# Expert blocks of 512, 256 and 128 tokens in a fused attention and routing kernel, with routing begun three steps sooner and TensorE begun on products of the identity

## The chip, the cores and the metric

The kernel runs on one core of one Trainium2 chip. The metric is the device time of one execution in microseconds, as the median of several runs. A profiled execution gives, besides, the order of time on each engine. In the profile PE is TensorE's matmuls, PEld its weight loads, DVE is VectorE, ACT is ScalarE, POOL is GpSimd, SP is SyncE, which here only issues DMAs; a "q" behind a name is the engine's sequencer, which waits and issues. L310 is line 310 of the kernel.

## The reference

Two stages are computed in fp32. The first is a gated attention without softmax for 8 batches of 2496 tokens, with 64 features for scores and 256 for values. The second sends each of the 19968 tokens to one of 8 experts, chosen by its id, and each expert is a pair of matrices with a relu between.

```python
scores = (1/S) * z @ z.T            # per batch, S = 2496, z: S x 64
attn   = np.maximum(scores, 0) ** 2
x      = u * (attn @ v)             # S x 256
...
expert_idx = token_ids * 2654435761 % 8
for e in range(8):
    h = np.maximum(x[expert_idx == e] @ w1[e], 0)   # 256 -> 1024
    out[expert_idx == e] = h @ w2[e]                # 1024 -> 256
```

## The kernel before

**Attention** (lines 731 to 842) goes through 200 steps: batch, group of 2 x 256 queries (5 a batch, the last of 2 x 224), block of keys (5 a group). In a step TensorE makes scores (`score`, L228), or ACT's queue loads them back from where the mirrored block was stored (`recall`, L289), since scores are symmetric; VectorE makes four sums of them (`sums`, L261 to L264) and a transposed copy for the mirror (`mirror`, L272). Then `attend` (L310) multiplies by v with the seven block products of a 2 x 2 scheme in place of eight. At the end of a group `join` (L320 to L328) puts the seven results together, reading the banks that the next group's first products need. VectorE prepares two steps ahead of TensorE. The scores of steps 0 and 1 and the transposes of z (`turn_z`, L171) stand ahead of the loop; the first score product is the first work of TensorE.

**Routing** (`places`, L415 to L604) is a generator: from step 5 on, each step of the attention runs one piece of it, 19 in all. It loads the ids (L424), counts the tokens of each expert by matmuls and scans, shares them out into blocks (`share`), finds the expert of each block (`eb_i`) and the slot of each token (`row`). A block belongs to one expert. There are as many blocks of 512 as surely can be filled, NL = 32; what is left of each expert goes into NR = 35 blocks of 128, which may be partly filled. `fill` zeroes the slots of the small blocks.

**Between the two** the rows of x are put into `xg_dram` and fetched back (`put`, `fetch`), multiplied by u on VectorE (`multiply`, L374) and scattered by POOL to their slots in `x_dram` (`sort`, L395). The last group goes another way: `gate_late` transposes it on TensorE against the identity (L384), multiplies it from PSUM (L386), and sorts it. The most frequent expert comes first in the slots, so the first two blocks (`SURE`) are surely complete before the last rows are sorted; their x is loaded five steps before the end (L814), and turned (`turn_x`, L697 to L705) at the last two steps (L789).

**Experts** (L989 to L1021): in iteration i TensorE multiplies block i by w1 (`up_large`, L901, "U") while block i-1 is multiplied by w2 (`down_large`, L931, "D"), each by seven block products. Upwards a product stands for two halves of the hidden features, so there are 14 pieces of U in an iteration, and 7 of D. Small blocks use plain products ("u" with L954, "d" with L965); `SMALL` gives each iteration but the first one or two of them. "X" and "x" turn the x of the next blocks. The order of the pieces is written out in `ORDER` as a string; engines are in order, so that string is the order on TensorE, VectorE and ScalarE. In `products` the seven products come as 1, 6, 7, 5, 2, 3, 4. Product 2 adds into the bank of 1, product 3 into the bank of 5:

```python
        ps1 = made(1, None)
        nc.scalar.copy(p1, ps1)                       # L864
        nc.vector.tensor_add(u, p1, made(6, None))    # L866
        ps7 = made(7, None)
        ps5 = made(5, None)
        nc.vector.tensor_add(c21, u, ps7)             # L871
        nc.vector.tensor_add(c22, c21, ps5)           # L872
        made(2, ps1)
        made(3, ps5)                                  # then L879
        nc.vector.tensor_sub(c21, c21, made(4, None)) # L882
```

For U four sums follow on VectorE (L912 to L915) when the next piece of U is asked for. Upwards the banks are two that are held (products 1 and 5) and two for the others; downwards two held, one for the others (6, 7 and 4 in turn), and one (`any`) for the small blocks and the gate. SP issues the weights in the order of the program, after the x loads of the same iteration (`load_x`, L684; `load_w`, L717, L720, L724). POOL stores the rows of the output by their indices (L854).

Of the kernel before, what the change touches and what calls it, by code (L numbers as in the profile page):

```python
# [11 lines left out]
F32 = mybir.dt.float32  # L12
# [13 lines left out]
def kernel(  # L26
# [26 lines left out]
    BLK = 512  # L53
    TB = BLK // P
    NL = -(-(N - E * (BLK - 1)) // BLK)
    NR = (N - NL * BLK + E * (P - 1)) // P
    NB = NL + NR
    NS = NL * TB + NR
# [317 lines left out]
    def gate_late(b, g, o):  # L376

        x_sb = late.tile([P, 2, 2, D], F32, name="x_row")
        for q in range(2):
            ps = down_ps.tile([P, 2, D], F32, name="g_ps", tag="any")  # L380
            for t in range(2):
                m = keys(g, t)
                for i in range(DP):
                    nc.tensor.transpose(ps[0:m, t, ts(i, P)], o[:, i, q, ds(t * P, m)], ident[:])  # L384
                x, y = times_u(b, g, x_sb, q, t, m)
                nc.vector.tensor_mul(x, ps[0:m, t].rearrange("p (h i k) -> p i h k", h=DP, k=L), y)  # L386
                sort(b, g, x_sb, 2 * q + t)
            yield
# [26 lines left out]
    def places():  # L415

        with tc.tile_pool(name="route", bufs=1) as route:
# [31 lines left out]
            def fill():  # L449
                if unfilled:  # L450
                    c = unfilled.pop(0)
                    n = min(7, NR - c)
                    nc.sync.dma_start(
                        x_dram[ds(NL * BLK + c * P, n * P), :].rearrange("(c p) d -> p c d", p=P), zero[:].unsqueeze(1).to_broadcast([P, n, D]))

# [58 lines left out]
            upto = wpool.tile([P, E, C], F32, name="upto", tag="w")  # L514
# [10 lines left out]
            nc.vector.tensor_tensor_scan(upto[:].rearrange(flat_e), one[:].to_broadcast([P, E * C]), upto[:].rearrange(flat_e), 0.0,  # L525
                                         op0=OP.mult, op1=OP.add)
            yield
            nc.vector.tensor_add(rank[:], rank[:], upto[:])
# [21 lines left out]

            large, large_end = share(count, BLK, 0, NL, "large")
            in_large = route.tile([P, E], F32)
            nc.vector.tensor_scalar(in_large[:], large[:], float(BLK), None, op0=OP.mult)
            nc.vector.tensor_sub(count[:], count[:], in_large[:])
            small, small_end = share(count, P, P - 1, NR, "small")
# [3 lines left out]
            shift = route.tile([P, E], F32)  # L559
            nc.vector.tensor_sub(shift[:], large_end[:], large[:])  # L560
            nc.vector.scalar_tensor_tensor(shift[:], shift[:], float(BLK), first[:], op0=OP.mult, op1=OP.subtract)
            more = route.tile([P, E], F32)
            nc.vector.tensor_sub(more[:], small_end[:], small[:])
            nc.vector.tensor_scalar(more[:], more[:], float(P), float(NL * BLK), op0=OP.mult, op1=OP.add)
            nc.vector.tensor_add(first[:], first[:], in_large[:])
            nc.vector.tensor_sub(more[:], more[:], first[:])
            nc.vector.tensor_sub(more[:], more[:], shift[:])

            for end, b0, nb in ((large_end, 0, NL), (small_end, NL, NR)):
# [4 lines left out]
                eb = route.tile([1, max(NL, NR)], F32, name="eb")  # L576
# [9 lines left out]
            past = upto  # L586
            nc.vector.tensor_tensor(past[:], rank[:], each(first), op=OP.is_ge)
            yield
            nc.vector.tensor_mul(past[:], past[:], each(more))
            yield  # L590
            nc.vector.tensor_add(rank[:], rank[:], each(shift))
            yield
            nc.vector.tensor_add(rank[:], rank[:], past[:])
            yield
# [78 lines left out]
    def large(j):  # L673
        return j < NL

    def slot_tiles(j):
        return range(j * TB, (j + 1) * TB) if large(j) else range(NL * (TB - 1) + j, NL * (TB - 1) + j + 1)

    def load_x(j):
        n = len(slot_tiles(j)) * P  # L680
        xq[j] = gpool.tile([P, n // L, DP, L], F32, name="xq" if large(j) else "xqs")
# [4 lines left out]
    def turn_x(j):  # L686

        n = len(slot_tiles(j))
        if large(j):
            x = gpool.tile([P, 2, DP, 2 * P], F32, name="xT")  # L690
            t = gpool.tile([P, 4, 2 * P], F32, name="xs")
# [3 lines left out]
        m = min(2, n) * P // L  # L695
# [12 lines left out]
    def turn_x_at_once(j):  # L708
        for _ in turn_x(j):
            pass  # L710

    def load_w(j, m):

        e = nc.sync.value_load(eb_i[0:1, j:j + 1], min_val=0, max_val=E - 1)
        if large(j):
# [13 lines left out]
    order.__enter__()  # L729

# [42 lines left out]
    for i, (b, g, s) in enumerate(steps):  # L773
# [14 lines left out]
        if i >= len(steps) - SURE:  # L788
            turn_x_at_once(i - len(steps) + SURE)  # L789
# [18 lines left out]
        if i == len(steps) - NT:  # L808
# [4 lines left out]
            for j in range(SURE):  # L813
                load_x(j)  # L814
        if i >= 5 and not is_routed:
# [4 lines left out]
        elif is_routed:  # L820
            if fetched and i >= fetched[0][0] + (5 if i < len(steps) - NT else 2):
                rows = fetched.pop(0)[1]
                multiply(*rows)
# [13 lines left out]
        if i == len(steps) - 2:  # L837
            load_u(b, g, late)
            load_w(1, 0)
# [46 lines left out]
    def up_large(j):  # L886
# [3 lines left out]
        h = hpool.tile([P, 2, 2, FQ, 2 * P], F32, name="h")  # L890
        sums = hpool.tile([P, 3, FQ, 2 * P], F32, name="hs")
        hid[j] = h, sums
        take = {1: (0, y11), 2: (2, y21), 3: (6, y22), 4: (3, t4), 5: (4, t1), 6: (5, t2), 7: (1, t3)}
        for f in range(0, FQ, 2):
            def made(m, ps):
                first = ps is None
                if first:
                    ps = up_ps.tile([P, 2, 2 * P], F32, name="h_ps", tag="held" if m in (1, 5) else "other")
# [5 lines left out]
            r = rpool.tile([P, 2, 2, 2 * P], F32, name="r")  # L904
# [12 lines left out]
    def down_large(j):  # L917
        h, sums = hid[j]
# [133 lines left out]
```

## Time and profile before

| | |
|---|---|
| runs | 2508.93, 2510.86, 2513.44 us (median 2510.86) |
| the profiled execution | 2507.8 us, its span 2506.0 us |
| busy: PE, PEld, DVE, ACT, POOL | 2476.4, 2110.9, 1653.4, 705.8, 548.9 us |
| mean granted TensorE clock | 0.998 |
| attention on TensorE, first to last | 7.26 to 1453.9 us |
| experts on TensorE, first to last | 1453.9 to 2497.9 us |
| DMA | 557.19 MB, mean 222 GB/s |

A line of the waits says who waited for whom, with the total in us, the number of waits and the longest. A line of the order of time has the start, the duration, the engine, the line, the operation, what it writes and reads, the shapes, the count (neighbours of one kind stand together), and in brackets the idle time of the engine before it with what ended it. A matmul in fp32 is recorded as two records, so a product of four records is two matmuls. Matmuls overlap their neighbours' ends, so the distance between starts is their price, not the duration.

### The profile page before, as it was taken

Reading aid. Unit: us, or ns where it says so; the run is one execution under the profiler, and the core shown is the slowest. Engines: PE = TensorE matmul, PEld = TensorE weight load, DVE = VectorE, ACT = ScalarE, POOL = GpSimd, SP = SyncE. Lnnn points to the kernel's source line nnn. Section 1 sums busy time; section 2 is a strip of 40 time slices with the busy share of each in tenths; the row PEclk is TensorE's granted clock in tenths of the full one; section 3 lists DMA queues with packets and bytes.
Section 4 is the critical chain, followed back from the end, with each engine's and each line's share of the span. In section 5 each row is a group of like instructions: output and inputs, shape, how many; then the busy total and the mean of one; then the engine's idle time right before and its main releaser. Section 6 shows DMA issues by size and latency. Waiting matters only on the chain.

```text
span 2506.0 us, 36968 instructions
## 1 busy us (share of the span) xinstructions
PE 2476.4 (99%) x13631; PEld 2110.9 (84%) x13631; DVE 1653.4 (66%) x3151; ACT 705.8 (28%) x1203; POOL 548.9 (22%) x532
## 2 busy tenths in 40 slices
PE   8999999999999999999999989999999999999998
PEld 6787787787787777877787889999999999999998
DVE  7798768768778677687687665545555555555553
ACT  4324324224223233133233112222222222222221
POOL 0000333322332233233223221111111111111112
PEclk9999999999999999999999999999999999999999
DMA  8776899798797897897888797766676667667762
GB/s 148 201 206 176 244 272 227 211 248 203 234 262 191 244 249 184 251 250 198 246 244 230 200 284 240 244 227 227 236 236 203 222 225 232 204 224 245 236 217 72
DMA packets 604661, 557.19 MB, mean 222 GB/s; under 512 B 287068, under 2 KB 544685, under 8 KB 594240
## 3 DMA queue, kind: packets, MB, share of 16 engines
q1 hardware_dynamic: 513984, 369.74, 54.6%
q10 hardware_dynamic: 63168, 97.86, 11.9%
q0 software_dynamic: 27328, 87.23, 10.0%
q8 instruction: 107, 1.75, 0.3%
q14 instruction: 74, 0.61, 0.1%
HBM read 375.55 MB, written 175.60 MB: 220 GB/s over the span
## 4 chain that ended last, share of the span: by engine, by line
PE 91%; DMA 5%; DVE 2%; issue 1%; SPq 0%; ACT 0%; POOL 0%; POOLq 0%; DVEq 0%; ACTq 0%
PE acc L310 42%; PE o_ps L931 16%; PE h_ps L901 15%; PE s_ps L228 8%; PE h_ps L954 5%; PE o_ps L965 5%; DMA a<-scores 3%; DMA u_sb<-in_u_dram 1%; DMA scores<-mirror 0%; DMA zn<-in_z_dram 0%; DVE x_row L374 0%; DVE t L261 0%; DVE t L262 0%; DVE t L263 0%; ACT a L242 0%
## 5 line engine op out<-in xcount | busy, mean ns | idle before, releaser
L242 ACT ACTIVATE a<-s_ps 128x512 f32<-128x512 f32 (+2 forms) x508 | 248.1, 579 | 736.5 <-PE s_ps L228 697.5
L310 PE MATMUL acc<-t,vc 128*128 128x256 f32 (+3 forms) x1600 | 402.6, 374 | 0.0
L310 PEld LDWEIGHTS acc<-a,v_sb 128*128 128x128 f32 (+1 forms) x1600 | 293.3, 190 | 125.0 <-issue 45.5
L310 PE MATMUL acc<-a,v_sb 128*128 128x256 f32 (+3 forms) x1600 | 382.6, 382 | 5.3 <-DVE o L322 5.2
L395 POOL DMA_INDIRECT x_slots<-x_row,row x160 | 192.3, 1202 | 849.7 <-DVE x_row L374 642.9
L310 PE MATMUL acc<-t,v_sb 128*128 128x256 f32 (+3 forms) x1600 | 369.7, 373 | 0.0
L310 PEld LDWEIGHTS acc<-t,vc 128*128 128x128 f32 (+1 forms) x1600 | 303.0, 190 | 34.5
L310 PEld LDWEIGHTS acc<-t,v_sb 128*128 128x128 f32 (+1 forms) x1600 | 303.5, 190 | 33.6
L261 DVE TENSOR_TENSOR t<-a 128x512 f32<-128x512 f32 (+1 forms) x200 | 134.5, 672 | 226.5 <-ACT a L250 162.0
L901 PE MATMUL h_ps<-xs,w 128*128 128x256 f32 x1024 | 258.1, 380 | 0.0
L931 PEld LDWEIGHTS o_ps<-w,h 128*128 128x128 f32 x2048 | 248.6, 192 | 6.5
L228 PE MATMUL s_ps<-zT 64*128 64x512 f32 (+1 forms) x960 | 241.4, 617 | 9.1 <-DVE zT L171 8.4
L931 PE MATMUL o_ps<-w,h 128*128 128x128 f32 x2048 | 249.3, 275 | 0.0
L908 ACT ACTIVATE h<-h 128x512 f32<-128x512 f32 x192 | 121.0, 630 | 349.1 <-DVE h L872 153.2
L854 POOL DMA_INDIRECT out_dram<-o_sb,idx x128 | 126.7, 990 | 420.8 <-ACT h L908 271.2
L272 DVE STREAM_TRANSPOSE mirror<-a 128x512 f32<-128x512 f32 x320 | 198.4, 677 | 6.6 <-DMA scores<-mirror 6.5
L310 PE MATMUL acc<-a,vc 128*128 128x256 f32 (+3 forms) x800 | 201.1, 374 | 0.0
L901 PE MATMUL h_ps<-xT,w 128*128 128x256 f32 x768 | 194.0, 382 | 1.2 <-DVE h L872 1.2
L901 PEld LDWEIGHTS h_ps<-xs,w 128*128 128x128 f32 x1024 | 178.5, 191 | 15.5
L931 PEld LDWEIGHTS o_ps<-w,hs 128*128 128x128 f32 x1536 | 186.4, 192 | 4.8
L931 PE MATMUL o_ps<-w,hs 128*128 128x128 f32 x1536 | 187.1, 275 | 0.0
L611 POOL DMA_INDIRECT slot_tokens<-token,addr x160 | 169.7, 1061 | 49.0 <-issue 48.1
(154 smaller groups left out, 2756.7 us busy)
## 6 DMA issues: line engine op xcount, KB each, us to landing
w<-w_blocks SPq DMA_DIRECT2D x64, 1792.0 KB, 11.3
scores<-mirror SPq DMA_DIRECT2D x276, 256.0 KB, 4.8
a<-scores ACTq DMA_DIRECT2D x48, 1024.0 KB, 5.8
w1s<-in_moe_w_dram SPq DMA_DIRECT2D x35, 1024.0 KB, 10.3
w2s<-in_moe_w_dram SPq DMA_DIRECT2D x35, 1024.0 KB, 11.5
a<-scores ACTq DMA_DIRECT2D x32, 896.0 KB, 7.3
w_blocks<-w POOLq DMA_DIRECT2D x16, 1792.0 KB, 8.1
u_sb<-in_u_dram SPq DMA_DIRECT2D x72, 256.0 KB, 5.2
```

The lines of the kernel that those rows point to most:

```text
L228: nc.tensor.matmul(to, z_h[:, ds(h * HS + s * W + j * P, P)], at, start=True, stop=True)
L242: nc.scalar.activation(to, at, AF.Relu, scale=1.0 / S)
L261: nc.vector.tensor_sub(t1, y12, y11)
L272: nc.vector.transpose(m[:, :, j, h].rearrange("p (n i) k -> p i n k", i=QB), a[:, j, h].rearrange("p (i t) q r -> p i (t q) r", t=2))
L310: nc.tensor.matmul(acc[k][:, half, 0:w], x[0:n, j, :], y[0:n, j], start=(first and j == 0 and half == 0), stop=(last and j == 1), skip_gro ...
L395: st = nc.gpsimd.indirect_dma_start(out=x_dram[:, :], out_offset=bass.IndirectOffsetOnAxis(ap=row[0:m, c:c + 1], axis=0), in_=x_sb[0:m, q, ...
L611: st = nc.gpsimd.indirect_dma_start(out=slot_dram[:, None], out_offset=bass.IndirectOffsetOnAxis(ap=addr[0:n, to:to + 1], axis=0), in_=tok ...
L854: st = nc.gpsimd.indirect_dma_start(out=out[:], out_offset=bass.IndirectOffsetOnAxis(ap=idx[:, col:col + 1], axis=0), in_=o, in_offset=Non ...
L901: nc.tensor.matmul(ps[:, r], w1[j][:, k, ts(f + r, P)], y, start=first and r == 0, stop=True, skip_group_check=True)
L931: nc.tensor.matmul(ps[:, t], x[:, f, ts(t, P)], w2_block(w2[j], k)[:, f], start=first and t == 0 and f == 0, stop=f == FQ - 1, skip_group_ ...
L954: nc.tensor.matmul(ps[:, i, :], w1[j][:, c, ts(f + i, P)], x[:, 0, c, 0:P], start=(c == 0), stop=(c == DP - 1))
L965: nc.tensor.matmul(ps[:], hid[j][:, f], w2[j][:, f, :], start=(f == 0), stop=(f == FP - 1))
```

## The change

Blocks come in three sizes: 32 of 512, 7 of 256 (`MID`), and 21 of 128. Those of 256 go through the same functions as the large ones (renamed `up_big`, `down_big`), with half the columns in each product upwards and one tile of rows in place of two downwards, and with the prepared weights of seven blocks. `BIG` gives the order: every fifth of the 39 is one of 256. Small blocks stand only in iterations where neither the block nor the one before is of 256, and one in the last. The routing shares out at three levels, in 23 pieces, from step 2 on. `gate_late` makes all its transposes at once, in the held banks, and multiplies at the second "G". The x of block 1 is loaded three steps later (after the sorts issued till then) and turned in iteration 1; the multiplication of the last row group but one by u stands ahead of the last `join`. Iteration 0 has U alone and G at other places, iteration 1 has no small block and an order of its own, the last iteration ends with the small block. Ahead of all, TensorE makes twelve 128 x 128 products of the identity in fp32, whose result nobody reads.

```diff
-    BLK = 512
-    TB = BLK // P
+    BLK, MID = 512, 256
+    TB, TM = BLK // P, MID // P
     NL = -(-(N - E * (BLK - 1)) // BLK)
-    NR = (N - NL * BLK + E * (P - 1)) // P
-    NB = NL + NR
+    NM = -(-(N - NL * BLK - E * (MID - 1)) // MID)
+    NR = (N - NL * BLK - NM * MID + E * (P - 1)) // P
+    NBIG = NL + NM
+    NB = NBIG + NR
...
     def gate_late(b, g, o):
         x_sb = late.tile([P, 2, 2, D], F32, name="x_row")
+        made = []
         for q in range(2):
-            ps = down_ps.tile([P, 2, D], F32, name="g_ps", tag="any")
+            made.append(down_ps.tile([P, 2, D], F32, name="g_ps", tag="held", bufs=2))
+            for t in range(2):
+                for i in range(DP):
+                    nc.tensor.transpose(made[q][0:keys(g, t), t, ts(i, P)], o[:, i, q, ds(t * P, keys(g, t))], ident[:])
+        yield
+        for q in range(2):
             for t in range(2):
                 m = keys(g, t)
-                for i in range(DP):
-                    nc.tensor.transpose(ps[0:m, t, ts(i, P)], o[:, i, q, ds(t * P, m)], ident[:])
                 x, y = times_u(b, g, x_sb, q, t, m)
-                nc.vector.tensor_mul(x, ps[0:m, t].rearrange("p (h i k) -> p i h k", h=DP, k=L), y)
+                nc.vector.tensor_mul(x, made[q][0:m, t].rearrange("p (h i k) -> p i h k", h=DP, k=L), y)
                 sort(b, g, x_sb, 2 * q + t)
-            yield
+        yield
...
+            for size, spare, limit, name in ((BLK, 0, NL, "large"), (MID, 0, NM, "mid"), (P, P - 1, NR, "small")):
+                n, end = share(count, size, spare, limit, name)
...
-            past = upto
-            nc.vector.tensor_tensor(past[:], rank[:], each(first), op=OP.is_ge)
-            yield
-            nc.vector.tensor_mul(past[:], past[:], each(more))
-            yield
-            nc.vector.tensor_add(rank[:], rank[:], each(shift))
-            yield
-            nc.vector.tensor_add(rank[:], rank[:], past[:])
-            yield
+            for past, (lowest, more, _) in ((past_mid, levels[1]), (upto, levels[2])):
+                nc.vector.tensor_tensor(past, rank[:], each(lowest), op=OP.is_ge)
+                yield
+                nc.vector.tensor_mul(past, past, each(more))
+                yield
+            nc.vector.tensor_add(rank[:], rank[:], each(levels[0][1]))
+            yield
+            for past in (past_mid, upto):
+                nc.vector.tensor_add(rank[:], rank[:], past)
+                yield
...
+    warm = mm_ps.tile([P, P], F32, name="warm", tag="mm")
+    for _ in range(12):
+        nc.tensor.matmul(warm[:], ident[:], ident[:], start=True, stop=True)
...
-        if i >= len(steps) - SURE:
-            turn_x_at_once(i - len(steps) + SURE)
+        if i == len(steps) - 2:
+            for _ in turn_x(0):
+                pass
+        if i == len(steps) - 1:
+            multiply(*fetched[0][1])
...
-            for j in range(SURE):
-                load_x(j)
-        if i >= 5 and not is_routed:
+            load_x(0)
+        if i >= 2 and not is_routed:
...
             load_u(b, g, late)
+            load_x(1)
             load_w(1, 0)
...
-    ORDER = {"": "UuUDUuUDUdUDU" "XUDXUDUxUDUUDU", "made": "UuUDUuUDUdUDU" "XUDXuUDUxuUDUUDU",
-             "next": "UuUDUuUDUdUDU" "XUDXUDUxUDUUxDU", "last": "UdUDUuUDUuUDU" "XUDXUDdUxUDUUDU",
-             "first": "UUUUGUUGUUUUUUUU", "second": "DUDUUDUUDUUDUU" "xXUuDUXUuDUxUU"}
+    ORDER = {"first": "UUUUGUUUGUUUUUUU", "second": "DXDXDUDUUDUUDUU" "UxUDXUUXUUUU",
+             "other": "UuUDUuUDUdUDU" "XUDXUDUxUDUUDU", "end": "DDDDDDDd"}
...
+    BIG, SMALL = [], []
+    large, mid, small = list(range(NL)), list(range(NL, NBIG)), list(range(NBIG, NB))
+    for i in range(NBIG):
+        BIG.append(mid.pop(0) if i % (NBIG // NM) == NBIG // NM - 1 and mid else large.pop(0))
+        long = BIG[-1] < NL and (not i or BIG[-2] < NL)
+        SMALL.append([small.pop(0)] if long and i > 1 and len(small) > 1 else [])
+    for i in range(NBIG - 1, 1, -1):
+        if small and not SMALL[i] and BIG[i] < NL:
+            SMALL[i].append(small.pop(0))
```

The part of `up_big` and `down_big` that differs is the size: every tile is cut to `half(j)` columns (256 or 128) upwards, and `for t in range(n)` with n of 2 or 1 downwards.

## The prediction

> **What bounds it now.** I read the page first (busy shares, then the chain that ended last), then TensorE's waits, then the order of time at the three places that the change touches: the first 20 us, the passage from attention to the experts, and one steady expert iteration.
>
> ```profile
> span 2506.0 us, 36968 instructions
> ...
> PE 91%; DMA 5%; DVE 2%; issue 1%; SPq 0%; ACT 0%; POOL 0%; POOLq 0%; DVEq 0%; ACTq 0%
> ```
>
> TensorE (PE) carries 91% of the chain; the rest is short. What TensorE itself waits for is a short list (total, times, longest):
>
> ```profile
> PE s_ps L228 <- DVE zT L171: 8.4, 2, 7.3
> PE g_ps L384 <- DVE x_row L386: 5.6, 2, 4.7
> PE acc L310 <- DVE o L322: 5.2, 7, 1.9
> PE h_ps L901 <- DVE h L872: 1.2, 1, 1.2
> ```
>
> With L228's wait for ScalarE (0.7) and L954's (0.3) that is all, some 21 us of 2506. From 1850 to 2400 us TensorE is busy 550.00 of 550 us. So the change can gain by fewer matmul passes or by those few waits, and it can lose by making a new wait where there is none now. Time goes against the profiled execution: 2507.8 us, its span 2506.0; the median of the runs, 2510.86, lies 3.1 above it, and I add my difference to the median.
>
> **Part 1: fourteen small blocks become seven of 256 tokens.** With N = 19968 the sizes give 32 blocks of 512 as before, 7 of 256, and 21 instead of 35 of 128. A product of a large block upwards takes 0.866 us (1719.13 to 1719.99 below), downwards 1.785; an iteration with one large and one small block is 31.62 us (the distance of the L965 rows), three distances with two large and three small blocks are 70.27, so small = 7.03 and large = 24.59. A block of 256 has 28 matmuls of 128 columns each way. Sixteen records of 128 columns take 1.785 us, so a matmul (two records) takes 0.223, and the block 56 x 0.223 = 12.5. Two small blocks take 14.06. Gain: 7 x 1.56 = **-10.9 us**.
>
> **Part 2: what VectorE does in the iteration after a block of 256.** An iteration multiplies block i upwards (U) while i-1 goes downwards (D). This is the second half of one today, TensorE, then VectorE:
>
> ```profile
> 1719.13 1.03 PE L901 MATMUL h_ps<-xs,w 128*128 128x256 f32 x4
> 1719.99 1.03 PE L901 MATMUL h_ps<-xT,w 128*128 128x256 f32 x4
> 1720.86 1.95 PE L931 MATMUL o_ps<-w,hs 128*128 128x128 f32 x16
> ...
> 1728.81 1.89 PE L901 MATMUL h_ps<-xT,w 128*128 128x256 f32 x8
> ```
>
> ```profile
> 1720.19 0.69 DVE L882 TENSOR_TENSOR h<-h,h_ps 128x512 f32<-128x512 f32 x1 [1.96 <-PE h_ps L901]
> 1720.80 1.30 DVE L697 STREAM_TRANSPOSE xT<-xq 128x512 f32<-128x512 f32 x2
> ...
> 1724.52 0.42 DVE L871 TENSOR_TENSOR o_sb<-ro,o_ps 128x256 f32<-128x256 f32 x1
> ...
> 1728.55 0.69 DVE L872 TENSOR_TENSOR h<-h,h_ps 128x512 f32<-128x512 f32 x1
> ```
>
> U4 ends at 1719.99. VectorE then works without a gap through L882, two transposes of the next x, four sums (L912 to L915), D5's two additions, four sums of x, U6's addition, the small block's transpose, and L871 and L872, to 1729.24, 9.25 us after U4. U3 adds into the bank that L872 reads; it is the second product of the row at 1728.81, so it is due at 1729.67. Margin: 0.43 us, and D5, D2 and D3 (5.36 us) are what gives it. Where D is of 256 tokens, these three last 2.68: U3 is due 5 x 0.866 + 2.68 = 7.01 us after U4. VectorE loses only half of D5's additions (0.86 to about 0.56, by the 0.28 us of a 128x128 row at L197), so its list ends after 8.95, and U3 starts at about 8.98. **A new wait of 1.97 us.** Small blocks are kept out of these iterations, so nothing else covers it. Six of the seven have the small transpose in the list (0.36); the seventh (i = 35) has not: 6 x 1.97 + 1.61 = **+13.4 us**. Bounds: 11 if D5's additions cost nothing, 15.5 if they cost what they do now. In the iteration of the 256 block itself the list is short instead (halved U work): 6.7 us against a U3 due at 5 x 0.446 + 3 x 1.785 = 7.6, no wait. Behind the waiting U3 stand D4, U4 and the whole next iteration on TensorE, so the wait goes into the end one for one.
>
> The weights are 3.58 MB for each block of 256 and arrive in time: an iteration after one lasts some 20 us and asks for 5.2 MB, 260 GB/s, and the trace holds 267 GB/s over 1700 to 1750.
>
> **Part 3: from attention to the experts.** Today the first expert product starts at 1453.9 and D1 of block 0 at 1476.0, with 4.7, 0.9 and 1.2 us of waits between. All eight transposes now come in one go, without waiting for the multiplication: these 5.6 us go. What is late next? D1 also needs w2 of block 0.
>
> ```profile
> 1457.56 0.36 SPq L717 DMA_DIRECT2D w<-w_blocks x1
> ...
> 1472.15 0.39 SPq L720 DMA_DIRECT2D w1s<-in_moe_w_dram x1
> ```
>
> The load issued at 1457.56 landed 14.4 us later, at 1471.9. The change puts the four loads of block 1's x in front of it and of block 1's w1. They wait for the four sorts before them on POOL (1452.00 to 1457.0 today, which follow the landing of both x blocks; with one x block, whose last load is issued at 1439.6 and lands some 8.6 later, they start near 1448.5), which land near 1455.6. Issues then go on to 1459.6, 2 us later than today, and w2 lands at about 1472.8. TensorE would be ready at 1471.9: with block 1's transposes gone, the multiplication by u stands in front of the join on VectorE and waits for its u (about 1455 against 1458.8), and in the second set of products U3 waits some 3 us for L872, because the four gate products (0.4 each) and the sums (2.5) lie before it. So D1 starts near 1472.8: -3.2, bounds -6.4 (ready at 1469.6, weights no limit) and 0. After it D6 and D7 stand side by side, and D7 waits for D6's addition in the one bank: +0.65 (0.2 after D6's end, then 0.42). In the second iteration's new order U3 is due 6.1 us after U4 and VectorE's list is 7.3: +1.25; the old wait of 0.34 goes. **-1.65**, from -4.9 to +1.6. Loads of block 2 wait for the last sorts as today (1472), 25 us ahead of their use.
>
> **Part 4: the end.** The last small block comes after the large one, not between D6 and D7.
>
> ```profile
> 2501.15 0.97 POOL L854 DMA_INDIRECT out_dram<-o_sb,idx x1 [0.30 <-issue]
> ```
>
> Four stores, 1.28 us apart, begin 1.39 us after D3 and hold the end 8.3 us beyond the last matmul. Now the small block's 3.45 us cover three of them: with five stores the last is issued 4.72 us after D4 and ends 4.85 later, 6.1 beyond the last matmul: -2.16. D7's wait for D6 (0.74) is uncovered: **-1.4**, from -2.2 to 0.
>
> **Part 5: the first products.** The scores start at 7.26 and advance by 0.855 us a matmul until 12.0, later by 0.48. The 12 products of the identity can start near 1.5. If they end the slow stretch, ScalarE begins 0.95 us sooner and this square moves from 12.19 to about 10.5:
>
> ```profile
> 12.19 1.23 DVE L246 TENSOR_TENSOR a<-a 128x1024 f32<-128x1024 f32 x1 [4.99 <-ACT a L242]
> ...
> 14.47 2.78 PE L228 MATMUL s_ps<-zT 64*128 64x512 f32 x8 [1.14 <-DVE zT L171]
> ```
>
> Behind it stand the transposes of z, whose last chunk lands at 13.06 and so allows 1.1 us of the 1.7. Twelve products last 2.7 us at the later pace, 4.8 at the slow one (0.223 x 0.855/0.48); today's slow stretch is 4.75 us of work. I take **-0.8**, from -1.1 to 0.
>
> The page's granted clock (9 in every slice) doesn't show this slow stretch. The Trainium skill, "TensorE: Matmul & The Clock Gate", section "Part 1: The HAM clock gate (the "warmup" mystery)", says TensorE starts at half clock and is released after some 3.4 us of activity in a free-running window. By that rule 4.8 us would be enough (-1.1) and 2.7 alone would not (0).
>
> **Part 6: routing.** It starts at step 2 and takes 23 pieces instead of 19: three more passes of 1.45 us and about 2.8 us of small operations on VectorE. VectorE has no gap from 146.7 to 194 us today, so this could cost. But the pieces come three steps sooner: in steps 15 to 19 they sum to 11.3 us against 13.95. The ten token loads move from 49.9 to about 42 on SP (12.9 us of issue); behind them stands one mirror's store, wanted 8 us later. Cost **0**, from -0.5 to +1.
>
> **Sum:** -10.9 + 13.4 - 1.65 - 1.4 - 0.8 = -1.35. 2510.9 - 1.4 = **2509.5**.
>
> **Rivals.** (A) The sum, 2504 to 2514 by its likelier ends: 0.55. (B) The wait after a 256 block is half as long or absent, if VectorE is further ahead than the list says: for it, VectorE is busy only 53% of 1850 to 2400; against it, that is an average, and the list above has no gap. Each microsecond saved there counts seven times: 2496 to 2503, chance 0.27. (C) Slower: VectorE's routing work doesn't fit in front of the join of the fourth row of blocks. L322 ends at 166.93 and TensorE begins the next group at 166.99; what VectorE is late there by more than 0.06 us, TensorE loses one for one, up to the whole addition of 7.2: 2516.7, chance 0.12. Against it stand the three steps. (D) The clock and the boundary don't respond (the products end too soon, w2 lands at 1476): +4.0 on A, 2513.5, chance 0.06.
>
> I call 0.2% (5 us) what can be told from no change. Faster by more: B's 0.25 and 0.08 of A. Slower: 0.10 of C and 0.05 of A. Within: 0.52. The range holds A's bounds and B's larger part: 2497 to 2517; A alone 2504 to 2514.
>
> **What would show it.** Right: TensorE's waits list U3 for L872 some seven times at about 2 us, in the iterations after 256 blocks alone; the busy share of TensorE falls there and nowhere else; g_ps no longer waits; the last store starts about 5 us after D4's end; score products at 0.48 us from the start. Wrong: no such waits (then B), or waits of L310 for L322 between 100 and 200 us (then C).

## The result, and the profile after

The changed kernel takes 2520.09 us (median of five runs, 2516.43 to 2522.37), the kernel before beside it 2509.09 (2507.46 to 2513.44): ratio 1.0039, 95% interval 1.0024 to 1.0053. That is 10 us slower, where 1.4 us faster was forecast, and outside the range of 2497 to 2517. The profiled execution is the fastest of the five: 2516.43 us, its span 2514.7, which is 8.7 us more than the span before. The ratio of 1.0039 is little more than 1 + 8.7/2506 = 1.0035, so most of the loss lies in that profile.

The page after, the span and the shares of the chain:

```profile
span 2514.7 us, 37414 instructions
...
PE 89%; DMA 4%; DVE 4%; issue 1%; SPq 1%; ACT 0%; POOL 0%; DVEq 0%; POOLq 0%; ACTq 0%
```

VectorE's share of the chain has doubled from 2% to 4%. TensorE's waits (total, times, longest) say where:

```profile
PE h_ps L929 <- DVE h L899: 13.2, 8, 1.8
PE acc L313 <- DVE o L325: 3.7, 3, 2.1
PE s_ps L231 <- DVE zT L174: 2.9, 3, 1.2
PE h_ps L929 <- issue: 2.5, 1, 2.5
PE g_ps L387 <- DVE o L331: 1.8, 1, 1.8
PE o_ps L960 <- DVE ro L893: 1.7, 2, 1.1
...
PE g_ps L387 <- DVE o L325: 1.1, 1, 1.1
```

(L901 and L872 of before are L929 and L899 here, L931 is L960, L228 and L310 are L231 and L313, L384 is L387, L322 is L325.) Seven of the eight waits of the first line are those that Part 2 forecast; the eighth (1.05 us) is in the second iteration, where Part 3 had reckoned 1.25. The wait of g_ps, which was to go, has moved from the multiplication to the join. To read the rest I cut both traces at places that TensorE passes in each: the first product of step 1 and of step 15, the last product of the attention, D1 of block 0, and the end of the last product of all. Differences of the profiled executions, after less before:

| stretch | before, us | after, us | difference | forecast |
|---|---|---|---|---|
| start to step 1 | 25.34 | 27.93 | +2.6 | -0.8 |
| step 1 to step 15 | 107.38 | 108.83 | +1.45 | 0 |
| step 15 to the end of attention | 1321.0 | 1322.1 | +1.1 | 0 |
| to D1 of block 0 | 22.30 | 20.97 | -1.3 | -3.2 |
| D1 to the last product | 1021.84 | 1028.84 | +7.0 | +4.8 |
| last product to the end | 8.15 | 5.99 | -2.2 | -2.2 |
| sum | 2506.0 | 2514.7 | +8.7 | -1.4 |

(The forecast's +4.8 is -10.9 + 13.4 + 0.65 + 1.25 - 0.34 + 0.74, the -2.2 its -2.16.) The experts and the end went nearly as reckoned; the start is the largest miss. The first 23 us of TensorE, after:

```profile
1.44 4.73 PE L752 MATMUL warm<-ident 128*128 128x128 f32 x24 [1.44 <-POOL ident masks.py:199]
7.37 4.40 PE L231 MATMUL s_ps<-zT 64*128 64x512 f32 x16 [1.20 <-DVE zT L174]
12.89 1.09 PE L231 MATMUL s_ps<-zT 64*128 64x512 f32 x2 [1.13 <-DVE zT L174]
14.56 2.88 PE L231 MATMUL s_ps<-zT 64*128 64x512 f32 x6 [0.57 <-DVE zT L174]
17.37 3.78 PE L313 MATMUL acc<-a,v_sb 128*128 128x256 f32 x8
```

In the kernel before, the same sixteen records of scores took 6.08 us:

```profile
7.26 6.08 PE L228 MATMUL s_ps<-zT 64*128 64x512 f32 x16 [7.26 <-DVE zT L171]
```

The products of the identity do what they were meant to do: the scores last 4.4 us. But TensorE is then done with them at 11.8, and the next chunks of z are not transposed: it idles for 1.13 and 0.57 us, after 1.20 ahead of the first scores. The first eight records of attention, the last row of the first of these views, take 3.57 us to the next, 0.45 each, where a_order below needs 0.23. The same stretch by times (us, then busy time of each engine, then the granted clock):

```profile
12.03:15.44 3.41, 1.98 (x6) 0.81 (x7) 2.66 (x6) 3.38 (x6) 0.00 (x0) 1.00 1.05 300
15.44:18.85 3.41, 3.41 (x8) 1.54 (x6) 3.34 (x8) 2.88 (x6) 0.00 (x0) 0.50 0.96 286
18.85:22.26 3.41, 3.41 (x10) 2.69 (x9) 3.38 (x7) 1.26 (x2) 0.00 (x0) 0.50 0.00 0
```

After 3.41 us in which TensorE was busy for 1.98 us, the clock is at half for two such stretches.

### The profile page after: what moved, and what is told of

It is laid out like the page before. It is cut to its first block, busy times and chain, and to the rows that moved or that the text cites. A ratio compares the mean times of both kernels' runs of the same rounds, so it can differ in the third digit from the quotient of the medians.

```text
span 2514.7 us, 37414 instructions
## 1 busy us (share of the span) xinstructions
PE 2478.1 (99%) x13767; PEld 2112.6 (84%) x13767; DVE 1715.5 (68%) x3350; ACT 723.0 (29%) x1259; POOL 542.2 (22%) x532
## 4 chain that ended last, share of the span: by engine, by line
PE 89%; DMA 4%; DVE 4%; issue 1%; SPq 1%; ACT 0%; POOL 0%; DVEq 0%; POOLq 0%; ACTq 0%
PE acc L313 43%; PE o_ps L960 16%; PE h_ps L929 15%; PE s_ps L231 9%; PE h_ps L983 3%; PE o_ps L994 3%; DMA a<-scores 2%; DMA u_sb<-in_u_dram 1%; SPq L707 1%; DVE xT L719 0%; DMA zn<-in_z_dram 0%; DVE x_row L377 0%; DVE h L899 0%; DVE hs L943 0%; DVE t L264 0%
## 5 line engine op out<-in xcount | busy, mean ns | idle before, releaser
L313 PE MATMUL acc<-t,vc 128*128 128x256 f32 (+3 forms) x1600 | 403.9, 375 | 0.0
L313 PEld LDWEIGHTS acc<-a,v_sb 128*128 128x128 f32 (+1 forms) x1600 | 294.8, 190 | 125.4 <-issue 53.0
L313 PE MATMUL acc<-a,v_sb 128*128 128x256 f32 (+3 forms) x1600 | 385.2, 384 | 4.5 <-DVE o L325 3.7
L313 PE MATMUL acc<-t,v_sb 128*128 128x256 f32 (+3 forms) x1600 | 369.7, 373 | 0.0
L313 PEld LDWEIGHTS acc<-t,vc 128*128 128x128 f32 (+1 forms) x1600 | 304.3, 190 | 34.6
L313 PEld LDWEIGHTS acc<-t,v_sb 128*128 128x128 f32 (+1 forms) x1600 | 303.4, 190 | 33.6
L929 PE MATMUL h_ps<-xs,w 128*128 128x256 f32 (+1 forms) x1248 | 287.8, 361 | 0.0
L960 PEld LDWEIGHTS o_ps<-w,h 128*128 128x128 f32 x2272 | 275.7, 192 | 8.5 <-DVE ro L893 2.1
L960 PE MATMUL o_ps<-w,h 128*128 128x128 f32 x2272 | 279.1, 275 | 1.7 <-DVE ro L893 1.7
L881 POOL DMA_INDIRECT out_dram<-o_sb,idx x142 | 139.9, 985 | 646.0 <-ACT h L936 461.1
L936 ACT ACTIVATE h<-h 128x512 f32<-128x512 f32 (+1 forms) x234 | 138.5, 592 | 389.6 <-DVE h L899 176.3
L231 PE MATMUL s_ps<-zT 64*128 64x512 f32 (+1 forms) x960 | 242.0, 613 | 4.3 <-DVE zT L174 2.9
L929 PE MATMUL h_ps<-xT,w 128*128 128x256 f32 (+1 forms) x936 | 217.0, 363 | 15.7 <-DVE h L899 13.2
L929 PEld LDWEIGHTS h_ps<-xs,w 128*128 128x128 f32 x1248 | 208.0, 191 | 16.3
L960 PEld LDWEIGHTS o_ps<-w,hs 128*128 128x128 f32 x1704 | 206.3, 192 | 6.3 <-DVE o_sb L899 1.7
L960 PE MATMUL o_ps<-w,hs 128*128 128x128 f32 x1704 | 210.2, 275 | 0.0
L313 PE MATMUL acc<-a,vc 128*128 128x256 f32 (+3 forms) x800 | 201.4, 374 | 0.0
L929 PEld LDWEIGHTS h_ps<-xT,w 128*128 128x128 f32 x936 | 163.3, 192 | 36.1 <-DVE h L899 16.4
```

Source lines behind the costliest of these rows:

```text
L231: nc.tensor.matmul(to, z_h[:, ds(h * HS + s * W + j * P, P)], at, start=True, stop=True)
L313: nc.tensor.matmul(acc[k][:, half, 0:w], x[0:n, j, :], y[0:n, j], start=(first and j == 0 and half == 0), stop=(last and j == 1), skip_gro ...
L881: st = nc.gpsimd.indirect_dma_start(out=out[:], out_offset=bass.IndirectOffsetOnAxis(ap=idx[:, col:col + 1], axis=0), in_=o, in_offset=Non ...
L929: nc.tensor.matmul(ps[:, r], w1[j][:, k, ts(f + r, P)], y, start=first and r == 0, stop=True, skip_group_check=True)
L936: lambda o, i, k, ps=None: nc.scalar.activation(o, o if ps is None else ps, AF.Relu))
L960: nc.tensor.matmul(ps[:, t], x[:, f, ts(t, P)], w2_block(w2[j], k)[:, f], start=first and t == 0 and f == 0, stop=f == FQ - 1, skip_group_ ...
```

## The experiments

All ratios are to the kernel before, run beside each on the same chip, with 95% intervals. The stretches are those of the table above, from one profile of each kernel; "step 1 at" is the first stretch.

| kernel | ratio | step 1 at | 1 to 15 | 15 to the end of attention | to D1 | D1 to last product |
|---|---|---|---|---|---|---|
| before | | 25.34 | 107.38 | 1321.0 | 22.30 | 1021.84 |
| after | 1.0039 (1.0024 to 1.0053) | 27.93 | 108.83 | 1322.1 | 20.97 | 1028.84 |
| a_order | 0.9973 (0.9964 to 0.9981) | 24.28 | 108.83 | 1324.5 | 22.48 | 1014.08 |
| a_nowarm | 1.0026 (1.0016 to 1.0037) | 25.79 | 108.84 | 1323.7 | 20.67 | 1028.27 |
| a_bridge | 1.0021 (1.0012 to 1.0029) | 25.63 | 108.84 | 1322.7 | 20.84 | 1028.85 |
| a_mult | 1.0026 (1.0017 to 1.0035) | 24.13 | 108.83 | 1326.1 | 22.19 | 1028.84 |
| b_warm | 1.0009 (1.0000 to 1.0018) | 28.48 | 107.38 | 1327.3 | 22.85 | 1021.84 |
| a_r3 | 1.0043 (1.0029 to 1.0057) | 28.47 | 106.07 | 1329.1 | 22.27 | 1028.83 |
| a_r3d | 1.0023 (1.0014 to 1.0032) | 24.12 | 106.08 | 1322.7 | 24.01 | 1028.82 |
| a_best | 0.9961 (0.9948 to 0.9974) | 26.00 | 106.08 | 1322.5 | 26.77 | 1014.07 |
| a_best2 | 0.9959 (0.9946 to 0.9973) | 24.54 | 106.08 | 1322.3 | 19.98 | 1015.84 |
| a_best3 | 0.9954 (0.9941 to 0.9967) | 24.39 | 106.08 | 1324.0 | 19.89 | 1013.47 |
| a_best_nw | 0.9956 (0.9943 to 0.9968) | 24.98 | 106.08 | 1324.5 | 22.15 | 1015.12 |

Four theories were to be told apart, one for each stretch that missed or held a wait: the seven waits come from VectorE's list; the start loses by a fallen clock; routing loses by its counts and by ending later; the passage loses by the multiplication in front of the join. The rival in each case is that the stretch is bound by something else anyway.

**The waits after a block of 256 (a_order).** One more order string, used where the block before is of 256:

```diff
+             "after": "UUDUUDUXUDXU" "UDUDUxUDUUDU"}
-        for p in ORDER[... else "end" if i == NBIG else "other"]:
+        for p in ORDER[... else "end" if i == NBIG else "after" if NL <= BIG[i - 1] < NBIG else "other"]:
```

> The changed kernel, with an order of its own for the iterations that follow a block of 256: the turns of the next x move from the second half to the first, so that VectorE's list behind U4 loses two transposes and four sums (about 2.2 us) while U3 is still due some 7.0 us after U4. Theory (the seven waits of U3 are made by what stands in VectorE's list, and nothing else covers them): the seven waits of 1.6 to 1.8 us all go, about -13.5 us, 2506.6, ratio to the kernel before 0.999. Rival (the waits come from the order of the products, the bank that the first product holds, and not from the length of the list): the waits stay, 2520. Between: the first half becomes late instead, and about half is won, 2513.

The wait as the changed kernel has it, TensorE and then VectorE:

```profile
1604.23 1.03 PE L929 MATMUL h_ps<-xT,w 128*128 128x256 f32 x4
1607.02 1.13 PE L929 MATMUL h_ps<-xT,w 128*128 128x256 f32 x4 [1.76 <-DVE h L899]
```

```profile
1598.80 1.30 DVE L719 STREAM_TRANSPOSE xT<-xq 128x512 f32<-128x512 f32 x2
...
1606.28 0.69 DVE L899 TENSOR_TENSOR h<-h,h_ps 128x512 f32<-128x512 f32 x1
```

VectorE works from the transposes to L899 without a gap; TensorE has nothing else to do from 1605.3 on. With the transposes and sums of x half an iteration earlier, all seven waits are gone. Of L929's waits for L899 this is what remains in a_order:

```profile
PE h_ps L929 <- DVE h L899: 1.0, 1, 1.0
```

That one is in the second iteration. D1 to the last product fell by 14.76 us, 2.1 for each wait, and the ratio by 0.0066. (That is more than the 0.999 expected; its profile also kept the clock at the start, as told below.) The theory holds: the length of VectorE's list made these waits, and the seven blocks of 256 then bring about what they were reckoned to bring.

**The start (a_nowarm, a_bridge, b_warm).** a_nowarm leaves the twelve products out; b_warm adds them, and nothing else, to the kernel before. a_bridge puts more of them where TensorE waited for z, and writes all of them to a bank of the attended products (`acc`) in place of one of the scores:

```diff
+    def keep_warm(n):
+        for _ in range(n):
+            nc.tensor.matmul(warm[:, 0, 0:P], ident[:], ident[:], start=True, stop=True)
+    keep_warm(12)
...
+                if (b, g, s) == (0, 0, 2) and j == 0:
+                    keep_warm(5 if h else 6)
```

> The changed kernel without the twelve products of the identity. Theory (the early products let TensorE finish the first scores before z is there, it idles, and the clock falls to half for 6.8 us while the first block is attended): without them the clock is released at about 12 us and stays, the second step starts at about 25.3 instead of 27.9, time 2517.5, ratio to the kernel before 1.003. Rival (the products are harmless and the start is late for another reason): 2520, and the second step still starts at 27.9.

> The changed kernel with eleven more products of the identity (0.22 us each), six and five of them ahead of the two halves of the third step's scores, where TensorE waited 1.2 and 1.1 us for the transposes of z. Theory (the clock falls because TensorE stands idle for too much of one stretch of 3.4 us): it stays at full speed from 5.2 us on, the first attended block lasts 6.0 us instead of 8.4, the second step starts at about 25.2 to 25.5, time 2517.4, ratio 1.0025. Rival (the clock falls for a reason that has nothing to do with idling here, or full speed at 15 us isn't to be had so early): the half clock from 15.4 us stays, 2520.

> The kernel before, with nothing added but the twelve products of the identity. Theory (whether the early start wins or loses hangs on where the stretches of 3.41 us lie by which the clock is set: with a stretch that holds most of TensorE's idling the clock falls and the second step starts 2.6 us later than before, without one it starts 1.1 us sooner): the runs are a mixture of both, the median between 2510.9 - 1.1 and 2510.9 + 2.6, ratio 0.9995 to 1.001. Rival 1 (the forecast's step: always a gain): -0.8, ratio 0.9997 with no run's start later. Rival 2 (always a loss): +2.6, ratio 1.001.

In a_bridge the clock stays at full from 6.8 us until after the start (it falls at 352), and step 1 starts 2.3 us sooner than in the changed kernel; in a_nowarm 2.1 us sooner. The first products of attention in a_bridge:

```profile
17.47 1.99 PE L315 MATMUL acc<-a,v_sb 128*128 128x256 f32 x8
```

So the theory holds for the traces. a_bridge's step 1 is still 0.3 us later than in the kernel before: the products in its second gap end 1.1 us after VectorE has z transposed. But the kernels that begin just as the changed kernel does don't all lose. This is a_order, whose start is not changed:

```profile
14.24 1.95 PE L231 MATMUL s_ps<-zT 64*128 64x512 f32 x6 [0.52 <-DVE zT L174]
16.12 1.99 PE L313 MATMUL acc<-a,v_sb 128*128 128x256 f32 x8
```

The same products at full clock; step 1 starts at 24.28, 1.06 us sooner than before, which is the forecast's -1.1. Of six profiles with the twelve products and nothing in the gaps, three kept the clock (a_order, a_mult, a_r3d: step 1 at 24.1 to 24.3) and three lost it (the changed kernel, b_warm, a_r3: 27.9 to 28.5). In b_warm, the products alone, eleven runs give +2.3 us (0 to 4.5). So a profiled execution gained 1.1 or lost 2.6 to 3.1 against the one profile of before; three kernels without the products (before, a_nowarm, a_best_nw) start step 1 at 24.98 to 25.79, so these sizes are good to some 0.4 us. Rival 1 of b_warm (always a gain) is refuted, and so is "always a loss". b_warm's profile is of its slowest run (2517.72 us of 2508.61 to 2517.72); how many of its runs lost the clock was not seen. The times of a_nowarm and a_bridge are below that of the changed kernel, but the intervals overlap, so their sizes are shown by the traces alone.

**Routing (a_r3, a_r3d).**

```diff
-        if i >= 2 and not is_routed:
-            is_routed = next(routed, True) is True
+        if i >= 3 and not is_routed:
+            for _ in range(2 if i in (20, 21) else 1):      # a_r3d; a_r3 has the first line only
+                is_routed = is_routed or next(routed, True) is True
```

> The changed kernel with routing begun at step 3 instead of 2. Theory (what the routing costs TensorE in steps 8 to 14 comes from its counting products, which take a bank that the scores of the same step want): one collision of the counts with scores instead of two, and the small count falls on a step without scores; the distance from the start of step 1 to that of step 15 goes from 108.83 back to about 107.4, -1.45. It ends one step later, at 25. Rival (VectorE's work is what costs there): 108.8 stays. Time 2518.7 by the first, 2520 by the second; the attention from step 15 on as in the changed kernel or some 2 us longer, since the sorts start later still.

> The changed kernel with routing begun at step 3 and two pieces of it run at each of the steps 20 and 21 (where the step prepared has no scores), so that it ends at step 23 as in the kernel before, in place of 24. Theory (the routing that ends later makes the sorts start later and crowds the DMA queues between 280 and 390 us, where TensorE waits for a recalled block or the transposed z of the next batch): besides the 1.45 of the counts, the distance from step 15 to step 50 goes from 250.6 to 254.0 (four profiles) back to the 248.4 of the kernel before, together -4 to -6: about 2515, ratio 1.002. Rival (those waits come and go from run to run and have nothing to do with the end of the routing): -1.45 alone, 2518.7.

The first half of the theory holds, and more than was expected: 108.83 becomes 106.07, in all six kernels begun at step 3. The counting products of the routing take one of the four banks that the scores use. TensorE's waits between 60 and 140 us, in the changed kernel and then in a_r3:

```profile
PE s_ps L231 <- ACT a L245: 1.4, 2, 0.7
```

```profile
PE s_ps L231 <- ACT a L245: 0.7, 1, 0.7
```

Step 9 of the changed kernel, with both counts and scores, lasts 9.91 us, 1.84 more than in the kernel before, where it has scores alone, and 0.68 of that is idle; the single small count makes step 7 0.95 longer. Whether they fall together hangs on the step at which routing begins: at 2 they do so three times (steps 7, 9 and 11), at 3 once. VectorE has the same pieces of routing in both, and TensorE waits for none of them here, which speaks against the rival.

The second half, that a later end crowds the queues, stays half open. The scatters of x by POOL do move. Between 300 and 400 us, in the changed kernel and then in a_r3d (the fifth busy time is POOL's, with the number of its instructions, and the last number GB/s):

```profile
300.00:400.00 100.00, 97.87 (x450) 80.08 (x449) 76.26 (x154) 26.09 (x46) 45.20 (x44) 0.98 0.96 298
```

```profile
300.00:400.00 100.00, 98.17 (x454) 78.62 (x453) 74.79 (x152) 30.27 (x52) 33.82 (x32) 1.00 0.95 267
```

Steps 15 to 50 take 248.4 to 250.3 us in the seven profiles where routing ends at step 23, 250.6 to 254.0 in the five where it ends at 24, 255.25 in the one at 25. But from step 50 to the end of attention the five are 2.9 us shorter on average than the seven, so most is given back: from step 15 on the table's column shows no difference between an end at 23 and one at 24. a_r3, with the end at 25, is the longest, 5.9 us above the median of the others, and its ratio is 0.0020 above a_r3d's, with intervals that overlap by a little. So a_r3 as a whole shows no gain over the changed kernel; an end that late probably costs, but that the changed kernel's does is not shown.

**The passage (a_mult).**

```diff
-        if i == len(steps) - 1:
-            multiply(*fetched[0][1])
...
-                if i < len(steps) - 1:
-                    multiply(*rows)
+                multiply(*rows)
```

> The changed kernel with the last multiplication by u put back behind the last join on VectorE. Theory (the join is late because VectorE waits for u in front of it): the join starts some 3.5 us sooner, TensorE's two waits for it at the last transposes (1.1 and 1.8) go, and the half clock that follows them with them; D1 of block 0 is then held by its w2 or by U3, so between -1 and -3.7: about 2518, ratio 1.003. Rival (the passage is bound by the weights or by U3 anyway): 2520, D1 at 1479.8 as it is.

In the changed kernel the join (L325) stands on VectorE behind the multiplication, and that behind its u:

```profile
1461.36 0.43 DVE L377 TENSOR_TENSOR x_row<-x_row,u_sb 128x256 f32<-128x256 f32 x1 [3.48 <-DMA u_sb<-in_u_dram]
1462.33 1.10 DVE L377 TENSOR_TENSOR x_row<-x_row,u_sb 128x256 f32<-128x256 f32 x3 [0.54 <-DMA u_sb<-in_u_dram]
1463.34 0.38 DVE L325 TENSOR_TENSOR o<-r,acc 128x224 f32<-128x224 f32 x1
```

In a_mult the join starts 0.9 us before the last product of attention does, not 4.5 us after it, and the transposes go through at once. But VectorE then waits for the same u ahead of U's additions, and TensorE behind it (VectorE first, then TensorE):

```profile
1462.69 0.43 DVE L377 TENSOR_TENSOR x_row<-x_row,u_sb 128x256 f32<-128x256 f32 x1 [1.79 <-DMA u_sb<-in_u_dram]
```

```profile
1462.66 1.04 PE L387 MATMUL g_ps<-ident,o 128*128 128x128 f32 x8
1463.53 1.03 PE L926 MATMUL h_ps<-xT,w 128*128 128x256 f32 x4
1467.53 2.07 PE L926 MATMUL h_ps<-xT,w 128*128 128x256 f32 x4 [2.97 <-DVE h L896]
```

The stretch to D1 is 22.19, with the clock at half twice there (3.4 us each) where it was once. That is no worse than the 20.97 of the changed kernel as far as can be told: the eight profiles with the changed kernel's passage (after, a_order, a_nowarm, a_bridge, a_r3, a_r3d, a_best2, a_best_nw) scatter from 19.98 to 24.01. Nor do the times tell: 1.0026 is what the theory forecast, and its interval overlaps the changed kernel's. What the trace shows is that the two waits for the join went and that as long a one came ahead of U3: with the multiplication at either place, the next thing on VectorE waits for u. So the rival is right that U3 (of the first set of products) holds the passage, but through u and not by itself; this rests on one trace.

**The cures together (a_best, a_best2, a_best3, a_best_nw).** a_best is a_order, a_bridge and a_r3d in one, with twelve identity products ahead of the transposes at the passage, written to their held bank:

```diff
+            for _ in range(0 if q else 12):
+                nc.tensor.matmul(made[q][:, 0, 0:P], ident[:], ident[:], start=True, stop=True)
```

> The changed kernel with four of the cures together: the order of its own after blocks of 256; the eleven identity products in the gaps of the first scores; routing from step 3 with two pieces at steps 20 and 21; and twelve more identity products ahead of the first transposes of the last row group, where TensorE waited 3 us for the join and the clock fell to half for 3.4 us. Theory (each of the losses was of its own): 2503.4 of the order alone, -1.6 for the start, -3 to -5 for routing, -1.7 for the clock at the passage: 2496 to 2498, ratio 0.995. Rival (order alone does it, the others are noise): 2503.

The seven waits are gone and routing has its 106.08; the start (26.00) is 1.9 us sooner than in the changed kernel but 0.7 later than in the kernel before, and the last cure failed. The held bank lies where the join still reads, so the products wait for it too, and then run at half clock:

```profile
1461.83 5.49 PE L388 MATMUL g_ps<-ident 128*128 128x128 f32 x24 [3.46 <-DVE o L333]
```

a_best2 drops them and has `keep_warm(2 if h else 4)`; a_best3 also has `"first": "UUUUGUUUUUUUGUUU"` (the second G behind U11, not U12 as its expectation says); a_best_nw is a_best2 without any product of the identity.

> The version with four cures, without the products ahead of the transposes at the passage (they waited for the join themselves, then ran 5.3 us at half clock in its place), and with four and two products in the gaps of the first scores in place of six and five (there the products ended 0.4 and 1.1 us after z was ready). Theory (those two sets of products cost, nothing else did): the passage from the last attended product to D1 of block 0 goes from 26.8 us to 21 to 24, the second step starts at 24.3 to 24.8 instead of 26.0, time 2501.5 - 5 = 2496.5, ratio 0.994. Rival (the clock falls again at the start, or the passage stays): 2500, ratio 0.996.

> The same, and in iteration 0 the multiplication of the last row group (the second G) moved from behind U7 to behind U12, so that its 1.4 us on VectorE stand behind the addition that U3 waits for and no longer in front of it. Theory (U3 of the second set waits 2.5 us because VectorE does the gate products and four sums first): U3 waits 1.1, D1 starts 1.4 us sooner, ratio 0.0005 lower than the kernel beside it. Rival (w2 of block 0 or the held bank then holds D1): no change, and TensorE waits ahead of D1 for weights or for the multiplication.

> The order of its own after blocks of 256 and routing from step 3 with two pieces at steps 20 and 21, without any product of the identity. Theory (the identity products gain 1 us when the clock stays and lose 2.6 when it falls, so on the whole they are worth nothing): within 1 to 2 us of the kernel with the products in the gaps, second step at 25.3 to 25.8, ratio 0.994 to 0.995. Rival (they gain, once the gaps are filled): 1 to 1.5 us more than it.

In a_best2 step 1 starts at 24.54, as expected, and the passage is 19.98 us, less than the 21 to 24 expected and the lowest of the scatter said above; the ratio, 0.9959, lies between the theory's 0.994 and the rival's 0.996, nearer to the rival, and the intervals don't part the four versions. a_best3's U3 waits 1.18 us in place of 2.50, and D1 starts at the same distance, since it now waits for w2:

```profile
PE o_ps L966 <- DMA w<-w_blocks: 2.4, 1, 2.4
```

(0.9 in a_best2.) So the rival is right: behind the join and VectorE the weights are next. a_best_nw, with no identity product, starts step 1 at 24.98 (25.3 to 25.8 was expected) and is as fast as the others: the products are worth nothing that can be told here. All four, and a_order alone, beat both kernels. But the intervals of the four overlap a_order's (0.9964 to 0.9981), so a_best's rival, that the order alone does it, is not refuted by times; the gain in routing and at the start is shown by the traces alone. The best median is a_best3's: ratio 0.9954 (0.9941 to 0.9967), 2495.6 against 2507.6 us.

## Why the prediction was wrong, point by point

The profile is 10.1 us above the forecast: 3.4 at the start (Part 5), 2.2 among the experts (Parts 1 to 4), 1.9 at the passage (Part 3), 1.45 in routing (Part 6), and 1.1 that is not settled. Some of the start's part is bad luck: had the clock held there, step 1 would have come at 24.1 to 24.3 in place of 27.93, and the kernel would still be some 5 us slower than before (an estimate from these rows).

- **Part 1, fewer matmuls: right.** D1 to the last product grew by 7.0; a_order puts 14.8 of it on the seven waits, and the waits of the second and last iteration make 2.4 (1.12 + 1.05 + 0.58 of idle, less the old 0.34). That leaves -10.2 for -10.9.
- **Part 2, the wait after a block of 256: right in place, number and size.** Seven waits, six of 1.76 and one of 1.62 us, in these iterations alone; with TensorE's restart they cost 14.8 by a_order, for +13.4 (11 to 15.5). Rival B, that VectorE runs further ahead, is out. The wait was reckoned at 1.97 and is 1.76; but it costs 2.1, more than the view shows. (The 0.28 us taken for a 128x128 addition is the time of the 96x128 rows at L197, the 128x128 ones take 0.25; in the changed kernel such an addition takes 0.28 to 0.29, so this did no harm.)
- **Part 3, the passage: failed in its step "these 5.6 us go".** The working had the multiplication wait for its u in front of the join on VectorE, but saw the landing of u at about 1455, and w2 as the last to come. u came at 1461.4 in an execution that was 5.1 us late there, so at about 1456.3 on the time scale of before; its last part and the multiplication took 2 us more. Its four loads were issued from 1456.2 to 1459.1, on that scale 1451.1 to 1454.0, so 1 to 2 us sooner than before and not four: the store of x ahead of them (L352) stood on SP 3.0 us behind a recalled block. TensorE so waits 1.1 and 1.8 us for the join in place of the 5.6, and the clock is at half for 3.41 us, from 1466.1 on. U3's wait (2.50) was foreseen. -1.3 came for -3.2; D6 and D7 cost 1.12 of idle, where 0.65 was reckoned.
- **Part 4, the end: right.** 5.99 us behind the last product, for 6.1; the last store is here:

```profile
2509.77 0.97 POOL L881 DMA_INDIRECT out_dram<-o,idx  x1 [0.30 <-issue]
```

- **Part 5, the identity products: the step that failed most, "I take -0.8, from -1.1 to 0".** The clock was released as reckoned and the square came sooner. (Twelve products were enough in all ten profiles that have them, full clock from 5.20 to 6.77. 4.8 us of work hold a whole stretch of 3.41 only if one begins in their first 1.4 us, which the working did not weigh.) -0.8 was forecast and +2.6 came. The bounds left out that TensorE, sooner done, stands idle until z lands, and that idling can take the clock away again: the gain (-1.1) holds only for the three profiles that keep it, the three others lose 2.6 to 3.1. The working had named z's last chunk as the next limit, and priced it as a smaller gain, not as a cause of loss.
- **Part 6, routing: wrong by +1.45.** The working counted VectorE's pieces, and these did no harm: between 100 and 200 us TensorE waits for ScalarE alone, 0.7 us, so rival C is out. What cost was on TensorE: the counting matmuls were not listed among what was moved, and they meet the scores in the four banks.
- **Steps 15 to the end of attention** differ by 1.1 between the two profiles; the thirteen profiles scatter here from 1321.0 to 1329.1, partly by half clock after waits near 350 and 385 us. Not settled.

Rival D's condition (clock and passage don't respond) came true in part, but it priced that at +4.0 on A; the clock did respond, and turned back. The mid blocks' loss by VectorE had eaten their gain, as forecast, so nothing was left to pay for the rest.

## What to carry to other kernels

A shorter block shortens the other engine's time to finish, so look at what its neighbour still has to do on VectorE, and move that half an iteration rather than giving up the block: here it was worth 14.8 us. An engine made ready sooner ahead of data that isn't there gains little, and TensorE can lose by it the clock it has won: here 1.1 us was won or 2.6 to 3.1 lost, and with the gaps filled the products were worth no more than none at all. When a generator of side work is shifted in time, list its instructions engine by engine, with the banks they take and what they meet there.

## What the runs showed of the hardware

The granted clock changed only at points 3.41 us apart in each execution, and where these lie differs from run to run: it became full at 5.20, 5.30, 5.45, 5.46, 6.33 and 6.51 us in six kernels with the same start. At the start the moment at which z lands counts too: with 5.45 b_warm lost the clock, where the last wait for z was 1.40 us, and with 5.46 a_r3d kept it, where it was 0.42. Whether it falls goes with how much TensorE worked between two such points, and no whole stretch of idling is needed. In the thirteen profiles, every such stretch at full clock with TensorE busy for 0.41 of it or less was followed by half clock, none above 0.58 was, and between these both happened. One wait of 2.13 us, at 352 us in the changed kernel, was enough (0.38 busy); 1.9 us at 381 in the kernel before was not (0.56). Half clock then lasted one or two stretches, until TensorE was busy for nearly the whole of one (0.86 at the least; 0.83 and once 0.94 were not enough, and at the start, in the table of times above, the first full one was not either). Why 0.42 to 0.58 goes both ways stays open; three of the six falls there (from 0.45, 0.49 and 0.58) came in the start, where score products use 64 of 128 rows.

The Trainium skill, "TensorE: Matmul & The Clock Gate", section "Part 1: The HAM clock gate (the "warmup" mystery)", gives a free-running window of 3413 ns, which agrees with these points. It has the clock go back after an idle window; here windows in which TensorE was busy for as much as 0.58 were enough.

A matmul that starts after a wait also costs more than the wait: U3's 1.76 us of idle set the stream back 2.03 us (4 records advance by 0.97 instead of 0.866 after it, and the last record before it ends 0.17 later than the next would have started).
